# New order tables for the five engines of a gated linear attention and relu-squared kernel

## The chip, the cores and the metric

The kernel runs on one core of a Trainium2 chip. The metric is the device time of one execution in microseconds, here the median of several runs. The five engines have one instruction list each and meet only at semaphores: TensorE (PE in the profile; its weight loads are the row PEld), VectorE (DVE), ScalarE (ACT), GpSimd (POOL) and SyncE (SP), which here only issues DMAs.

## The reference

Two layers are computed one behind the other. The first is a gated linear attention, a recurrence over the tokens; the second is a dense layer pair with a squared relu between:

```python
for t in range(S):                       # B, H, S, D = 4, 8, 768, 48
    state = alpha[:, :, t, :, None] * state + np.einsum('bhd,bhe->bhde', k[:, :, t], v[:, :, t])
    y[:, :, t] = np.einsum('bhd,bhde->bhe', q[:, :, t], state)
x = y.transpose(0, 2, 1, 3).reshape(3072, 384)
h = x @ w_in                             # 384 x 2048
r = np.maximum(h, 0.0)
out = (r * r) @ w_out                    # 2048 x 384
```

Inputs and output are float32; q, k, v and alpha have the shape 4 x 8 x 768 x 48.

## The kernel before

The tokens are cut into units of 256: four batches by three pieces, twelve units, the first pieces of all batches first. A unit g passes through these steps. In the tables the names carry the unit, and often a half or a block behind it, so that sq4_3 is the squaring of unit 4 that ends with block 3.

- **Loads.** lda, ldk, ldq, ldv fetch alpha, k, q and v (384 KB each, L460) into one of four RAW buffers. SyncE issues all of them but those of unit 2, which GpSimd issues, as it does the weights: win0, win1, wout0, wout1 (L433). ldv1 waits for q of unit 0, win for alpha of unit 1, unit 2's loads for v of unit 1, and unit 3's for wout0.
- **Front.** Unit 0 works by halves of the heads: ln0_0 and ln1_0 take logarithms (L476), m10_0 and m11_0 sum them on TensorE (L482 to L488), ei, ea and ec are exponentials, ekm and eqm scale k and q (L512), tr and et transpose them through PSUM (L524, L531, L533). Unit 1 works by token: ln1 (L538), m11 (L542 to L548), ei1, ea1, ec1, ekm1 (L643), eqm (L638), tr0_1 and tr1_1 (L666) with the evictions et0_1 and et1_1 (L674 on VectorE, L676 on ScalarE). From unit 2 on: pr multiplies alphas by pairs (L567 on VectorE, L569 on GpSimd), ln is its logarithm (L570), m1i and m1s sum on TensorE (L576), bk and aq (L594, L596, L605) and lm, lb, es make the other decays, ekm and eqm follow, and from unit 3 on two DMA transposes issued by SyncE, tr0 and tr1 (L654), put them in place. vc is v as bfloat16 (L633 on GpSimd, L634 on ScalarE).
- **Attention.** p0_g are the score matmuls (L874) with the state products (L727). mk0 and mk1 mask them (L891); sa, sc and sd carry the state from one unit of a batch to the next (L825 or L827, L837, L847). y is the output (L754, L762), xe and xf evict it (L908, L910), xt transposes it, on TensorE for units 0 to 3 (L926, with xv as its eviction, L938 or L940), by DMA from unit 4 on (L932).
- **Dense layers.** s1_g_u is one of eight blocks of the first layer (six matmuls, L989) into a hidden PSUM bank. re is the relu (L997 on ScalarE, L999 on VectorE), sq squares two blocks at once, or one for the last two (L1007 on VectorE, L1010 on GpSimd, L1011 on ScalarE). s2_g_j_s is a quarter of the second layer for one half of the unit's tokens (four matmuls, L1035), oe evicts it (L1042, L1044) and out stores it (L1051). The last unit ends with L950, L955, L957 and L958.

A hidden bank is used again two blocks later, or three where psO helps in units 0 and 1, so a block's matmuls wait for the relu of an earlier one.

The order is written out by hand in TABLES: one list of names for each engine. `arrange` (L86) gives every operation to the engine in whose list it stands; many have forms for several engines. `place` (L122) works out which waits are left, and `emit` (L173) writes each list as it stands. So an operation that isn't ready holds all that stands behind it in its list. A name like +512 is a filler: a matmul of a zero tile with 512 columns into psO (L1083), which stands among the first operations of TensorE's list.

Of the kernel before, what the change touches and what calls it, by code (L numbers as in the profile page):

```python
# [204 lines left out]

TABLES = {
    "act": """
        table ln0_0 ln1_0 ei0_0 xcaus ea0_0 ei1_0 ea1_0 ec1_0 et00_0 ec0_0 vc0 ln1 et01_0 et11_0 ei1 ea1 xe0 xv0
# [4 lines left out]
        re4_3 vc6 xe5 lm7 ln7 re4_7 oe3_1 re4_4 ei7 ea7 ec7 re4_6 sq4_6 es7 oe4_0 re5_0 re5_1 lm8 ln8 xe6 re5_2
        re5_3 ei8 ea8 re5_4 re5_5 es8 re5_6 re5_7 sq5_7 re6_0 re6_1 re6_2 vc8 oe5_0 xe7 lm9 ln9 re6_5 re6_6
        oe5_1 re6_7 ei9 ea9 es9 oe6_0 vc9 re7_0 lm10 re7_1 ln10 xe8 re7_3 ei10 ea10 re7_4 re7_5 es10 re7_6 re7_7
        re8_0 oe7_0 re8_1 re8_2 lm11 ln11 xe9 re8_3 re8_4 ei11 ea11 re8_5 re8_6 sq8_5 es11 sq8_7 re9_0 oe8_0
        vc11 re9_1 oe8_1 xe10 re9_3 re9_4 re9_5 re9_6 re9_7 re10_0 oe9_0 re10_1 re10_2 xe11 oe9_1 re10_3 re10_4
# [8 lines left out]
        oe1_1 sd3 sq2_7 sq2_6 xf3 lb5 ekm5 eqm1_5 eqm0_5 sa4 mk1_4 mk0_4 re3_2 pr6 sc4 sq3_1 xf4 sq3_3 re3_5
        sq3_6 lb6 ekm6 sa5 mk0_5 sc5 mk1_5 eqm0_6 eqm1_6 oe3_0 xf5 sq4_1 re4_5 pr7 sq4_3 sq4_7 sq4_5 bk7 lb7
        eqm0_7 sa6 eqm1_7 ekm7 sc6 sd6 mk0_6 mk1_6 pr8 oe4_1 xf6 sq5_3 bk8 lb8 ekm8 sq5_5 sq5_6 sa7 mk0_7 sc7
        mk1_7 eqm0_8 eqm1_8 sq6_1 re6_3 sd7 sq6_3 pr9 xf7 re6_4 sq6_5 sq6_6 sq6_7 bk9 lb9 ekm9 eqm0_9 eqm1_9
        mk0_8 sa8 mk1_8 oe6_1 pr10 sq7_1 xf8 re7_2 sq7_3 bk10 lb10 sq7_5 ekm10 sq7_6 sq7_7 sa9 mk0_9 eqm0_10  # L230
        eqm1_10 mk1_9 pr11 oe7_1 xf9 sq8_3 bk11 lb11 ekm11 sq8_6 re8_7 sa10 mk0_10 eqm0_11 eqm1_11 mk1_10 re9_2
        sq9_1 xf10 sq9_3 sq9_5 sq9_6 sa11 sq9_7 mk0_11 mk1_11 sq10_1 xf11 sq10_3 sq10_5 sq10_6 sq10_7 sq11_1
        sq11_3 sq11_5 sq11_6 sq11_7 oe11_11
    """,
    "pe": """
        +512 +512 +512 +512 +512 +512 +512 +512 m10_0 m11_0 +512 +512 +256 +256 tr00_0 +512 +256 tr10_0 +512
        +256 +256 tr01_0 p0_0 tr11_0 kv0 +512 +512 +512 +256 +256 p1_0 m11 +512 +256 y0 +512 +512 +256 tr0_1 xt0
# [4 lines left out]
        s2_1_1_3 y3 m1i5 s2_2_0_0 s2_2_0_1 xt3 s2_2_0_2 s2_2_0_3 s1_3_0 p0_4 s2_2_1_0 s2_2_1_1 s2_2_1_2 s2_2_1_3
        s1_3_2 s1_3_1 y4 s1_3_4 s1_3_3 m1i6 s1_3_6 s1_3_5 s2_3_0_0 s2_3_0_1 s1_3_7 p0_5 s2_3_0_2 s1_4_0 s1_4_1
        s2_3_0_3 s1_4_2 s1_4_3 y5 s2_3_1_0 s1_4_5 s2_3_1_1 s2_3_1_2 s1_4_7 s2_3_1_3 s1_4_4 m1i7 s2_4_0_0 s1_4_6
        s2_4_0_1 s2_4_0_2 p0_6 s2_4_0_3 s1_5_1 s1_5_0 s2_4_1_0 s2_4_1_1 s1_5_2 s2_4_1_2 s2_4_1_3 y6 s1_5_3 m1i8
        s2_5_0_0 s1_5_4 s1_5_5 s2_5_0_1 s1_5_6 s1_5_7 p0_7 s2_5_0_2 s1_6_0 s1_6_1 s2_5_0_3 s1_6_2 s1_6_3 y7
# [868 lines left out]
```

## Time and profile before

| | |
|---|---|
| median of 3 runs | 174.84 us |
| lowest, highest | 172.93, 175.71 us |
| span of the profiled execution | 171.8 us |
| time of the profiled execution | not given beside its span |
| TensorE, VectorE, ScalarE, GpSimd busy | 165.6, 118.2, 108.9, 24.2 us |
| bytes read, written | 25.17, 4.72 MB |
| granted TensorE clock, mean | 1.000 |

The page's DMA row shows the sixteen DMA engines busy at nine tenths or more almost without a break up to some 130 us, and little after that:

```
DMA  5999999999999999998999998999999582050012
```

Times in the views are microseconds from the start of the span; each row gives start, duration, engine, line and operation, tiles, shapes, and in a bracket how long the engine was idle before and what ended that.

### The profile page before, as it was taken

Reading aid. Unit: us, or ns where it says so; the run is one execution under the profiler, and the core shown is the slowest. Engines: PE = TensorE matmul, PEld = TensorE weight load, DVE = VectorE, ACT = ScalarE, POOL = GpSimd, SP = SyncE. Lnnn points to the kernel's source line nnn. Section 1 sums busy time; section 2 is a strip of 40 time slices with the busy share of each in tenths; the row PEclk is TensorE's granted clock in tenths of the full one; section 3 lists DMA queues with packets and bytes.
Section 4 is the critical chain, followed back from the end, with each engine's and each line's share of the span. In section 5 each row is a group of like instructions: output and inputs, shape, how many; then the busy total and the mean of one; then the engine's idle time right before and its main releaser. Section 6 shows DMA issues by size and latency. Waiting matters only on the chain.

```text
span 171.8 us, 5397 instructions
## 1 busy us (share of the span) xinstructions
PE 165.6 (96%) x2377; PEld 128.9 (75%) x2377; DVE 118.2 (69%) x207; ACT 108.9 (63%) x210; POOL 24.2 (14%) x33
## 2 busy tenths in 40 slices
PE   7999999999999999999999999999999999999994
...
DMA  5999999999999999998999998999999582050012
GB/s 143 323 298 186 260 316 219 245 245 288 182 234 209 269 173 211 305 217 146 288 168 211 267 192 153 337 178 243 255 211 205 81 103 85 0 141 0 22 69 92
DMA packets 74743, 33.37 MB, mean 194 GB/s; under 512 B 71648, under 2 KB 71904, under 8 KB 74720
## 3 DMA queue, kind: packets, MB, share of 16 engines
...
q0 software_dynamic: 1536, 4.72, 12.4%
...
HBM read 25.17 MB, written 4.72 MB: 174 GB/s over the span
## 4 chain that ended last, share of the span: by engine, by line
PE 58%; DMA 20%; SPq 7%; DVE 6%; ACT 4%; POOL 2%; issue 2%; DVEq 0%
PE psWH L989 25%; PE psO L1035 24%; DMA raw<-in_alpha_dram 7%; DMA wout<-in_moe_w_out_dram 6%; DMA raw<-in_q_dram 4%; SPq L460 3%; DMA raw<-in_k_dram 3%; SPq L654 3%; PE psX L950 2%; POOL raw L460 2%; DVE pm L891 1%; PE psZ L762 1%; PE psX L874 1%; DVE qks L638 1%; DVE qks L643 1%
## 5 line engine op out<-in xcount | busy, mean ns | idle before, releaser
L989 PE MATMUL psWH<-xt,win 128*128 128x256 bf16 x552 | 70.9, 274 | 0.4 <-ACT rr L997 0.3
L989 PEld LDWEIGHTS psWH<-xt,win 128*128 128x128 bf16 x552 | 63.2, 144 | 5.2 <-ACT rr L997 1.1
L1035 PE MATMUL psO<-wout,gt 128*128 128x384 bf16 x352 | 66.7, 326 | 0.0
L997 ACT ACTIVATE rr<-psWH 128x512 bf16<-128x512 f32 x79 | 46.8, 597 | 24.4 <-PE psWH L989 22.9
L1035 PEld LDWEIGHTS psO<-wout,gt 128*128 128x128 bf16 x352 | 32.7, 98 | 16.7 <-DMA wout<-in_moe_w_out_dram 0.2
L1007 DVE TENSOR_TENSOR gt<-rr 128x1024 bf16<-128x1024 bf16 (+1 forms) x46 | 26.6, 584 | 22.0 <-ACT rr L997 21.9
L891 DVE TENSOR_TENSOR pm<-psZ,caus 128x1024 bf16<-128x1024 f32 x12 | 14.6, 1218 | 4.7 <-PE psWH L727 4.1
L1042 ACT ACTIVATE osb<-psO 128x384 f32<-128x384 f32 x17 | 8.3, 491 | 11.7 <-PE psO L1035 11.3
L891 DVE TENSOR_TENSOR pm<-psX,caus 128x1024 bf16<-128x1024 f32 x12 | 14.6, 1218 | 1.0 <-PE psX L874 0.5
L1010 POOL TENSOR_TENSOR gt<-rr 128x1024 bf16<-128x1024 bf16 x3 | 5.7, 1894 | 58.7 <-ACT rr L997 58.7
L643 DVE TENSOR_TENSOR qks<-raw,ek 128x768 bf16<-128x768 f32 x11 | 10.5, 952 | 3.0 <-DMA raw<-in_k_dram 2.5
L638 DVE TENSOR_TENSOR qks<-raw,eq 128x384 bf16<-128x384 f32 x22 | 11.4, 553 | 1.7 <-ACT eq L613 1.0
L1083 PE MATMUL psO<-zero 128*128 128x512 bf16 (+1 forms) x33 | 9.1, 407 | 1.3 <-DVE zero L382 1.3
L999 DVE TENSOR_SCALAR rr<-psWH 128x512 bf16<-128x512 f32 x13 | 8.9, 687 | 1.6 <-PE psWH L989 1.4
L1011 ACT ACTIVATE gt<-rr 128x512 bf16<-128x512 bf16 (+1 forms) x11 | 9.1, 823 | 0.7 <-DVE rr L999 0.4
L910 DVE CAST xbf<-psZ 128x384 bf16<-128x384 f32 x10 | 5.5, 554 | 3.2 <-PE psZ L754 3.2
L634 ACT ACTIVATE vbf<-raw 128x768 bf16<-128x768 f32 x7 | 5.9, 843 | 2.2 <-DMA raw<-in_v_dram 2.1
L567 DVE TENSOR_TENSOR prd<-raw 128x384 f32<-128x384 f32 x9 | 5.7, 636 | 2.1 <-DMA raw<-in_alpha_dram 2.0
L609 ACT ACTIVATE la<-raw 128x384 f32<-128x384 f32 x8 | 4.2, 524 | 4.5 <-DMA raw<-in_alpha_dram 4.5
L570 ACT ACTIVATE lab<-prd 128x384 bf16<-128x384 f32 x10 | 5.2, 521 | 2.4 <-DVE prd L567 2.3
L847 POOL TENSOR_TENSOR sbd<-tmp,acm 128x192 bf16<-128x192 f32 x5 | 2.9, 583 | 25.8 <-DVE tmp L837 22.7
L908 ACT ACTIVATE xbf<-psX 128x384 bf16<-128x384 f32 x11 | 5.3, 482 | 1.9 <-PE psZ L754 1.9
...
## 6 DMA issues: line engine op xcount, KB each, us to landing
...
```

The costliest lines, as they stand in the source:

```text
L460: load_op[g, nm] = add(ring, lambda e, dst=dst, src=src: e.dma_start(dst, src), cost, (L_PRIO[g] + j if ring == "sp" else W_PRIO[2] + 10 * ...
L638: add("dve", lambda e, j=j, dst=dst: e.tensor_tensor(dst, RAW[r][:, 2, :, j, :].rearrange("p (n x) d -> p n x d", x=2), EQ[la][:, j].rearr ...
L643: add("dve", lambda e, a=a, E=E: e.tensor_tensor(QKS[qs][:, a, :, :, 0:D], RAW[r][:, 1 + a].rearrange("p h j d -> p j h d"), E[la][:].rear ...
L891: add("dve", lambda e, hf=hf, psT=psT: e.tensor_tensor(PM[pm][:, hf].rearrange("p r n j t -> p (r n) (j t)"), psT[:, :, :].rearrange("p r ...
L989: ins = pe.matmul(psN[:, i * T:(i + 1) * T], WIN[:, kk, hidden(fj)], mov, start=(kk == 0), stop=(kk == KT - 1))
L997: add("act", lambda e, psN=psN, rr=rr: e.activation(rr, psN, AF.Relu), act_ns(512), pu + 600, reads=[keyN], writes=[("rr", rb, half)], nam ...
L999: alts={"dve": (lambda e, psN=psN, rr=rr: e.tensor_scalar(rr, psN, 0.0, None, ALU.max), dve_ns(512))})
L1007: add("dve", lambda e, dst=dst, sq=sq: e.tensor_tensor(dst, sq, sq, ALU.mult), 148 + k * 267, pu + 1200, reads=[("rr", rb, h) for h in ran ...
L1011: "act": (lambda e, dst=dst, sq=sq: e.activation(dst, sq, AF.Square), act_ns(k * 512))})
L1035: ins = pe.matmul(psS, GT[gt][:, fj, j, :], WOUT[:, fj, :], start=(fj == 0), stop=(fj == FT - 1))
L1042: add("act", lambda e, j=j, psS=psS: e.activation(OSB[ob][:, j], psS, AF.Copy), act_ns(DM), ps_ + 700, reads=[keyS], writes=[("osb", ob, j ...
L1083: pr.arrange(TABLES, lambda n: lambda pe: pe.matmul(psO[:, 0:n], ZERO[:, 0:128], ZERO[:, 0:n], skip_group_check=True), zero)
```

## The change

Only the five lists change. All operations stay, with the same 33 fillers (23 of 512 columns, 10 of 256). 45 operations go from ScalarE to VectorE and 36 from VectorE to ScalarE; 25 go from VectorE to GpSimd and 7 from ScalarE to GpSimd; 6 go from GpSimd to VectorE and 2 from GpSimd to ScalarE. Every DMA stays on its queue, SyncE's or GpSimd's, but its place in it can change. The diff, cut to the lines spoken of below:

```diff
     "act": """
-        table ln0_0 ln1_0 ei0_0 xcaus ea0_0 ei1_0 ea1_0 ec1_0 et00_0 ec0_0 vc0 ln1 et01_0 et11_0 ei1 ea1 xe0 xv0
-        ec1 vc1 sa1 re0_0 re0_1 sq0_1 re0_3 xe1 re0_4 re0_5 ln2 re0_6 sq0_6 ei2 ea2 ec2 vc2 re1_2 es2 re1_3
+        table ln0_0 ei0_0 ln1_0 ea0_0 ei1_0 ea1_0 et00_0 et10_0 ec0_0 xcaus ec1_0 ln1 et01_0 et11_0 ei1 ea1 ec1
+        xe0 et0_1 vc1 et1_1 re0_0 re0_3 re0_2 xf1 re0_4 ln2 sq0_1 ei2 re0_6 ea2 sq0_6 re1_0 ec2 re1_3 es2 re1_4
...
     "dve": """
-        eqm0_0 ekm1_0 eqm1_0 et10_0 mk0_0 sa0 mk1_0 ekm1 eqm0_1 eqm1_1 sc0 et0_1 et1_1 mk1_1 mk0_1 sc1 re0_2 xf1
-        sq0_3 pr2 xv1 sq0_5 re0_7 re1_0 re1_1 ekm2 sq0_7 aq2 eqm0_2 eqm1_2 re1_5 et1_2 sq1_1 sq1_5 re1_7 mk1_2
-        pr3 sq1_7 sc2 mk0_2 bk3 eqm1_3 ekm3 aq3 pr4 eqm0_3 xv2 bk4 lb4 ekm4 eqm1_4 eqm0_4 sq2_1 mk1_3 mk0_3 sc3
...
+        ekm1_0 eqm1_0 mk0_0 sa0 zlb1 mk1_0 ekm1 eqm1_1 eqm0_1 sc0 xv0 sa1 mk0_1 mk1_1 re0_1 xe1 pr2 zlb0 sc1 xv1
+        re0_5 re0_7 bk2 eqm1_2 ekm2 re1_1 re1_2 aq2 sd1 sq1_1 eqm0_2 et1_2 re1_7 sa2 sq1_5 mk1_2 sc2 mk0_2 xe2
+        oe0_1 sd2 aq3 eqm1_3 eqm0_3 ekm3 bk4 lb4 ekm4 eqm0_4 eqm1_4 oe1_1 mk0_3 sc3 mk1_3 sd3 sq2_6 xf3 lb5 xv3
...
     "pe": """
-        +512 +512 +512 +512 +512 +512 +512 +512 m10_0 m11_0 +512 +512 +256 +256 tr00_0 +512 +256 tr10_0 +512
-        +256 +256 tr01_0 p0_0 tr11_0 kv0 +512 +512 +512 +256 +256 p1_0 m11 +512 +256 y0 +512 +512 +256 tr0_1 xt0
-        tr1_1 +512 +512 +512 +512 +512 +256 p0_1 s1_0_0 s1_0_1 s1_0_3 s1_0_2 y1 s1_0_4 s1_0_5 xt1 s1_0_6 s1_0_7
-        m1i2 s1_1_0 s1_1_1 s1_1_2 m1s2 s1_1_3 s1_1_4 tr0_2 s1_1_6 s1_1_5 tr1_2 s2_0_0_0 s1_1_7 p0_2 s2_0_0_1
...
+        +256 +512 +512 +256 +512 +256 +512 +256 +512 +512 +512 +512 +512 +512 m10_0 +256 +512 +512 +512 m11_0
+        +512 tr00_0 tr10_0 +512 +256 tr01_0 +512 p0_0 tr11_0 +256 +256 kv0 +512 p1_0 m11 +512 +512 +256 +512 y0
+        +256 +512 tr0_1 +512 xt0 tr1_1 +512 p0_1 s1_0_0 s1_0_3 s1_0_1 s1_0_2 y1 s1_0_4 xt1 s1_0_6 s1_0_5 m1i2
+        s1_0_7 s1_1_0 s1_1_1 s1_1_2 s1_1_3 m1s2 tr0_2 s1_1_4 s1_1_6 s1_1_5 s2_0_0_0 tr1_2 s1_1_7 s2_0_0_1 p0_2
...
     "pool": """
-        slinc slstr sident scaus scaus1 win0 win1 lda2 sd0 ldq2 ldv2 ldk2 wout0 sd1 wout1 bk2 sd2 sq2_3 vc4 pr5
-        bk5 sd4 vc5 bk6 sd5 sq5_1 vc7 sq8_1 vc10
+        scaus1 slinc slstr sident scaus vc0 win0 win1 lda2 ldk2 ldq2 ldv2 wout0 sq0_3 wout1 sq0_5 sd0 vc2 sq1_3
+        sq0_7 sq1_6 pr3 pr4 bk3 pr5 sq2_1 vc4 sq2_3 sq2_7 bk5 pr6 sd4 vc5 sq4_3 vc6 sq4_5 pr8 vc7 sq6_1 sq6_3
+        sd7 pr10 vc9 pr11 sd6 sq8_3 bk11 vc11 sq9_3 sq10_1 sq10_3 sq10_7 sq11_1
     """,
     "sp": """
-        lda0 ldk0 ldq0 ldv0 lda1 ldk1 ldv1 ldq1 lda3 ldk3 ldq3 lda4 ldv3 ldk4 ldq4 ldv4 tr0_3 tr1_3 lda5 tr0_4
-        out0_1 tr1_4 ldk5 ldq5 ldv5 lda6 ldk6 tr1_5 tr0_5 out2_1 xt4 ldq6 out1_1 ldv6 lda7 ldq7 ldk7 tr0_6 tr1_6
-        xt5 ldv7 out3_1 lda8 ldk8 tr0_7 tr1_7 out4_1 xt6 ldq8 ldv8 lda9 ldq9 ldk9 tr0_8 tr1_8 xt7 ldv9 lda10
...
+        lda0 ldk0 ldq0 ldv0 lda1 ldq1 ldv1 ldk1 lda3 lda5 lda4 ldk3 ldq3 ldq4 ldv4 ldv3 ldk4 tr1_3 tr0_3 out0_1
+        tr1_4 tr0_4 ldk5 ldq5 lda6 ldk6 ldv5 out1_1 tr1_5 tr0_5 xt4 out2_1 ldq6 lda7 ldv6 ldk7 ldq7 tr0_6 tr1_6
+        xt5 ldv7 lda8 ldk8 out3_1 tr0_7 tr1_7 xt6 out4_1 lda9 ldq8 ldv8 ldk9 ldq9 tr1_8 tr0_8 xt7 lda10 ldv9
...
```

More of the change, by code (lines that the diff above doesn't have):

```diff
@@ L213 @@
[L213 to L217, printed above, removed]
@@ new lines @@
+        oe2_1 xf4 xe4 ei6 re3_4 lm6 ea6 ec6 sq3_3 re3_6 sq3_5 sq3_6 re3_7 es6 re4_0 sq3_7 re4_2 re4_3 xe5 ln7
+        re4_5 ei7 ea7 ec7 lm7 oe3_1 sq4_7 sq4_6 oe4_0 es7 re5_0 re5_2 re5_1 lm8 ln8 xe6 sq5_1 re5_4 ei8 ea8
+        re5_5 re5_7 sq5_6 sq5_7 oe5_0 re6_0 re6_1 es8 lm9 ln9 re6_3 ei9 vc8 xf7 ea9 re6_4 re6_5 oe5_1 re6_6
+        re6_7 oe6_0 es9 ln10 ei10 re7_2 ea10 xf8 oe6_1 lm10 re7_4 xe8 sq7_5 re7_6 sq7_7 sq7_6 oe7_0 re8_1 re8_0
+        es10 re8_2 ln11 xf9 re8_4 vc10 re8_5 re8_6 lm11 re8_7 ei11 sq8_7 ea11 re9_0 oe8_0 es11 re9_1 re9_3 sq9_1
@@ L220 @@
+        re9_2 re9_4 xf10 re9_6 sq9_6 re10_1 re10_3 re10_2 xe11 sq10_5 re10_7 re10_6 re11_1 re11_3 re11_4 sq11_3
+        sq11_5 sq11_6 sq11_7
     """,
     "dve": """
-        zero zlinc zlstr zident zcaus zcaus1 zla0 zla1 zones zown zown0 zown1 zqk0 zqk1 zqk2 zlb0 zlb1 ekm0_0
-        eqm0_0 ekm1_0 eqm1_0 et10_0 mk0_0 sa0 mk1_0 ekm1 eqm0_1 eqm1_1 sc0 et0_1 et1_1 mk1_1 mk0_1 sc1 re0_2 xf1
-        sq0_3 pr2 xv1 sq0_5 re0_7 re1_0 re1_1 ekm2 sq0_7 aq2 eqm0_2 eqm1_2 re1_5 et1_2 sq1_1 sq1_5 re1_7 mk1_2
@@ L225 @@
-        pr3 sq1_7 sc2 mk0_2 bk3 eqm1_3 ekm3 aq3 pr4 eqm0_3 xv2 bk4 lb4 ekm4 eqm1_4 eqm0_4 sq2_1 mk1_3 mk0_3 sc3
[L226 to L233, printed above, removed]
+        zero zlinc zlstr zident zcaus zcaus1 zla0 zla1 zones zown zown0 zown1 zqk0 zqk1 zqk2 ekm0_0 eqm0_0
+        ekm1_0 eqm1_0 mk0_0 sa0 zlb1 mk1_0 ekm1 eqm1_1 eqm0_1 sc0 xv0 sa1 mk0_1 mk1_1 re0_1 xe1 pr2 zlb0 sc1 xv1
@@ L242 @@
[L242 to L246, printed above, removed]
@@ new lines @@
+        +256 +512 tr0_1 +512 xt0 tr1_1 +512 p0_1 s1_0_0 s1_0_3 s1_0_1 s1_0_2 y1 s1_0_4 xt1 s1_0_6 s1_0_5 m1i2
+        s1_0_7 s1_1_0 s1_1_1 s1_1_2 s1_1_3 m1s2 tr0_2 s1_1_4 s1_1_6 s1_1_5 s2_0_0_0 tr1_2 s1_1_7 s2_0_0_1 p0_2
+        s2_0_1_0 s2_0_1_1 s2_0_0_2 s2_0_1_2 s2_0_0_3 m1i3 s2_0_1_3 y2 s2_1_0_0 m1s3 xt2 s2_1_0_1 s2_1_0_2 m1i4
+        s1_2_0 s1_2_1 s2_1_0_3 s1_2_2 s1_2_3 s2_1_1_0 s2_1_1_1 s1_2_4 s1_2_5 s2_1_1_2 s2_1_1_3 p0_3 s2_2_0_0
+        s1_2_7 s1_2_6 m1i5 s2_2_0_1 y3 s2_2_0_2 xt3 s2_2_0_3 p0_4 s2_2_1_0 s1_3_0 s1_3_1 s2_2_1_1 s2_2_1_2
@@ new lines @@
+        s2_6_0_3 p0_8 s2_6_1_0 s1_7_1 s1_7_0 s2_6_1_1 s1_7_3 s2_6_1_2 s1_7_2 m1i10 y8 s2_6_1_3 s1_7_4 s1_7_5
+        s2_7_0_0 s1_7_6 s1_7_7 s2_7_0_1 p0_9 s2_7_0_2 s2_7_0_3 s1_8_1 s1_8_0 s2_7_1_0 s1_8_3 s2_7_1_1 s2_7_1_2
+        s1_8_2 s2_7_1_3 y9 m1i11 s1_8_4 s1_8_5 s2_8_0_0 s1_8_6 s2_8_0_1 s1_8_7 p0_10 s2_8_0_2 s1_9_0 s2_8_0_3
+        s1_9_1 s1_9_2 s2_8_1_0 s1_9_3 s2_8_1_1 s2_8_1_2 s2_8_1_3 s1_9_4 y10 s2_9_0_0 s1_9_5 s1_9_6 s2_9_0_1
+        s1_9_7 p0_11 s2_9_0_2 s1_10_0 s1_10_1 s2_9_0_3 s1_10_2 s1_10_3 y11 s2_9_1_0 s2_9_1_1 s1_10_4 s1_10_5
@@ L267 @@
+        ldk10 tr1_9 tr0_9 out5_1 out6_1 xt8 ldq10 lda11 ldk11 ldv10 tr0_10 tr1_10 xt9 ldv11 ldq11 tr1_11 tr0_11
+        xt10 out7_1 out8_1 xt11 out10_1 out9_1 out11_0 out11_10 out11_11
     """,
```

35 lines of the change are left out of this document (17 added, 18 removed).

## The prediction

> **What bounds the kernel now.** I read the page's head first, with the busy shares and the chain of waits by engine, then the busy time by stage (stretch, its length, then TensorE's busy time), then the rests ahead of single TensorE instructions.
>
> ```profile
> span 171.8 us, 5397 instructions
> ...
> PE 165.6 (96%) x2377; PEld 128.9 (75%) x2377; DVE 118.2 (69%) x207; ACT 108.9 (63%) x210; POOL 24.2 (14%) x33
> ...
> PE 58%; DMA 20%; SPq 7%; DVE 6%; ACT 4%; POOL 2%; issue 2%; DVEq 0%
> ```
> ```profile
> 140.00:150.00 10.00, 10.00 (x161) 7.97 (x160) 5.70 (x9) 4.80 (x9) 0.00 (x0) 1.00 0.22 61
> ```
>
> The 96% count the fillers of the start as work. The useful dense stretch begins with the scores of unit 1 (p0_1, at 17.32, below). From there TensorE hardly rests; the stage from 140 to 150 is full. Every rest after 17.32 that the timeline marks on TensorE is here, picked from several stretches, with the idle time in the bracket:
>
> ```profile
> 21.94 1.51 PE L989 MATMUL psWH<-xt,win 128*128 128x256 bf16 x12 [0.32 <-ACT rr L997]
> 41.49 0.34 PE L576 MATMUL psWH<-lab,linc 128*128 128x384 bf16 x1 [0.17 <-ACT lab L570]
> 61.52 0.37 PE L762 MATMUL psZ<-vbf,pm 64*128 64x48 bf16 x16 [0.38 <-DVE pm L891]
> 80.83 0.38 PE L874 MATMUL psX<-kqt 64*64 64x128 bf16 x13 [0.40 <-ACT eq L613]
> 88.80 0.34 PE L576 MATMUL psWH<-lab,linc 128*128 128x384 bf16 x1 [0.24 <-ACT lab L570]
> ```
>
> They add up to 0.32 + 0.17 + 0.38 + 0.40 + 0.24 = 1.51 us. Over a quarter of the chain of waits is DMA and SyncE's queue, but with rests this small TensorE's own work bounds the kernel from 17.32 on. The change keeps every matmul, so an order can win these 1.5 us and what it takes off the start; it can lose any amount by letting TensorE wait.
>
> **Part 1, the start.** Both versions issue 33 fillers, but ahead of unit 0's first decay sum m10_0 there were eight of 512 columns and now there are ten of 512 and four of 256, in width 12 for 8. The rows are picked from the timelines of TensorE, ScalarE and VectorE:
>
> ```profile
> 1.26 3.59 PE L1083 MATMUL psO<-zero 128*128 128x512 bf16 x8 [1.26 <-DVE zero L382]
> 4.94 0.26 PE L482 MATMUL psX<-laf,linc 128*128 128x192 bf16 x1
> 9.31 0.84 ACT L538 ACTIVATE laf<-raw 128x768 bf16<-128x768 f32 x1 [0.34 <-DMA raw<-in_alpha_dram]
> 10.00 1.04 PE L1083 MATMUL psO<-zero 128*128 128x512 bf16 x5
> 14.43 0.62 PE L666 MATMUL psZ<-ident,qks 128*128 128x128 bf16 x8
> 17.32 0.42 PE L874 MATMUL psX<-kqt 64*64 64x128 bf16 x16
> 16.19 0.84 ACT L634 ACTIVATE vbf<-raw 128x768 bf16<-128x768 f32 x1
> 29.38 1.02 ACT L676 ACTIVATE kqt<-psZ 128x1024 bf16<-128x1024 bf16 x1
> 31.26 0.68 DVE L674 COPY kqt<-psZ 128x1024 bf16<-128x1024 bf16 x1
> ```
>
> The eight took 3.59 / 8 = 0.45 us each and ended at 4.85, 0.09 before m10_0, so nothing covers four more. Later fillers take 1.04 / 5 = 0.21 us. The added four cost 4 x 0.21 = 0.83, less the 0.09, so 0.7 us, if the fast pace holds from 4.85; at 0.45 they cost 1.7. I take 0.7, and keep 1.7 for the range. The Trainium skill (TensorE: Matmul & The Clock Gate, Part 1) says that the slow pace lasts for a time of some 3.4 us of activity and not for a number of matmuls, give or take 0.5 us by the phase of a free-running window; by it the added fillers run mostly fast, which is the 0.7, or in a late phase up to 1.7; the trace agrees so far as eight took 3.59 us and all later ones ran fast.
>
> ScalarE passes the 0.7 on: ei0_0 now stands ahead of ln1_0, and et10_0 came over, so ln1 (L538, 9.31) is reached some 0.7 us later, and with it et11_0, p1_0, m11 and the front of unit 1. Then the two evictions et0_1 and et1_1 move from VectorE (0.68 each) to ScalarE (1.02 each), with the cast vc1 (0.84) between them. The rows for the two forms are those of unit 2's evictions. The first can start at the end of tr0_1, 14.43 + 0.62 + 0.7 = 15.75; 1.02 + 0.84 + 1.02 with two overlaps of 0.1 ends at 18.43, and p0_1 starts near 18.48 in place of 17.32: **+1.15 us**. The second half of win hides some of it:
>
> ```profile
> 9.58 1.71 POOL L433 DMA_DIRECT2D win<-in_moe_w_in_dram  x2 [6.64 <-DMA raw<-in_alpha_dram]
> DMA to landing us min/median/max: 8.5/9.9/11.3
> ```
>
> Issued near 10.5, the second piece lands 11.3 later, at 21.8; the idle 0.32 us ahead of 21.94 is this transfer (the bracket names a relu that had long ended), and a late TensorE no longer waits for it. Net **+0.85 us**.
>
> **Part 2, work moved to GpSimd.** Thirty-two operations come to GpSimd, eight leave; fourteen squarings of 1,024 columns stand there where there were three. TensorE waits for them only through GT, with slack. The price is what they do to VectorE:
>
> ```profile
> 122.56 1.89 POOL L1010 TENSOR_TENSOR gt<-rr 128x1024 bf16<-128x1024 bf16 x1 [34.92 <-ACT rr L997]
> 124.40 1.15 POOL L633 CAST vbf<-raw 128x768 bf16<-128x768 f32 x1
> 123.58 1.30 DVE L567 TENSOR_TENSOR prd<-raw 128x384 f32<-128x384 f32 x1 [0.41 <-DMA raw<-in_alpha_dram]
> 23.20 0.56 DVE L567 TENSOR_TENSOR prd<-raw 128x384 f32<-128x384 f32 x1 [0.39 <-DMA raw<-in_alpha_dram]
> 84.98 1.90 POOL L1010 TENSOR_TENSOR gt<-rr 128x1024 bf16<-128x1024 bf16 x1 [14.42 <-ACT rr L997]
> 85.19 1.22 DVE L891 TENSOR_TENSOR pm<-psZ,caus 128x1024 bf16<-128x1024 f32 x1
> ```
>
> The product pr11 started 0.88 us before GpSimd's squaring ended at 124.45, and took 1.30 in place of 0.56: it stood still until then. The mask at 85.19, whose first input is PSUM, ran beside a squaring at its usual 1.22. And vc10, up at 124.40, took 1.15 behind pr11, whose last 0.47 us it met. So a VectorE operation with both inputs in SBUF doesn't run beside one of GpSimd, and a squaring there can hold one of VectorE for up to 1.9 us. Three places where that decides, with the rows that show how much lies between VectorE's result and TensorE's use of it today (ln2 and m1i2; ekm2 and tr0_2; eqm0_2 with eqm1_2, and tr1_2):
>
> ```profile
> 23.98 0.52 ACT L570 ACTIVATE lab<-prd 128x384 bf16<-128x384 f32 x1
> 24.94 0.33 PE L576 MATMUL psWH<-lab,linc 128*128 128x384 bf16 x1
> 27.36 0.95 DVE L643 TENSOR_TENSOR qks<-raw,ek 128x768 bf16<-128x768 f32 x1
> 28.68 0.61 PE L666 MATMUL psZ<-ident,qks 128*128 128x128 bf16 x8
> 29.15 1.03 DVE L638 TENSOR_TENSOR qks<-raw,eq 128x384 bf16<-128x384 f32 x2
> 30.45 0.61 PE L666 MATMUL psZ<-ident,qks 128*128 128x128 bf16 x8
> ```
>
> (a) sq0_3 on GpSimd starts when re0_2 ends; y1, xe1 and then pr2 follow, so that pr2 comes up about 0.7 us later (an estimate from these steps' lengths) and waits the other 1.2. The log ln2 (23.98) and m1i2 (24.94) stand behind; between the end of the log and m1i2 lie 24.94 - 24.50 = 0.44 today, and VectorE's xv1 and re0_5 are late too, so about 0.6 of the 1.2 reach TensorE. (b) sq0_5 starts at the end of re0_5; bk2, now on VectorE ahead of ekm2, waits about 1.0, and ekm2 feeds tr0_2 with 28.68 - 28.31 = 0.37 between them today: 0.6 is not covered, with re1_1 and re1_2 queued behind, whose hidden banks s1_1_4 and s1_1_5 need: 0.3 more. (c) sq1_3, sq0_7 and sq1_6 (1.89, and two of half the columns, 0.95 each as an estimate from it) meet aq2, sd1, sq1_1 and eqm0_2, and eqm0_2 feeds tr1_2, with 0.27 between them today. If VectorE's queued operations go first, (c) costs nothing and the sum is 1.5; if GpSimd's go in between each time, (b) grows by 0.9 and (c) costs about 2.9, together 5.3. Pr11 got going at 124.45 though vc10 was up at 124.40, so the row is nearer to VectorE first: I take **2.3**, and keep 0 (if all is covered) and 5.3 for the range.
>
> **Part 3, the loads.** On SyncE lda5 moves ahead of lda4, ldk3 and ldq3, one more 384 KB transfer before them:
>
> ```profile
> 35.00 2.24 SPq L460 DMA_DIRECT2D raw<-in_v_dram  x1
> 39.62 1.28 SPq L460 DMA_DIRECT2D raw<-in_v_dram  x1
> 41.38 4.00 SPq L654 DMA_TRANSPOSE kqt<-qks  x2
> 80.67 0.58 SPq L1051 DMA_DIRECT2D out_dram<-osb  x1
> 50.61 1.00 POOL L569 TENSOR_TENSOR prd<-raw 128x384 f32<-128x384 f32 x1 [1.87 <-DMA raw<-in_alpha_dram]
> ```
>
> A load takes 1.3 to 2.2 us of the queue, so ekm3, eqm0_3, eqm1_3 and the transposes of 41.38 come that much later. Behind these transposes wait out0_1 and the transposes of unit 4, which p0_3 and p0_4 need. But p0_3 stands two groups later in TensorE's list (some 1.5 us, as the pair at 21.94), and TensorE is late by 0.85 + 2.3 there anyway: zero; without that cover up to 0.7. Likewise k5. lda8 passes out3_1 (80.67, 0.58), while pr8 behind it goes to GpSimd (1.00 for 0.56, +0.44): the two nearly cancel. A late TensorE absorbs rests that hang on transfers, at most 0.17 + 0.38 + 0.40 + 0.24 = 1.19; since the transposes wait for VectorE too, I count half: **-0.6**.
>
> **The rest at nothing.** Forty-five operations go from ScalarE to VectorE and 36 back, mostly relus and evictions. The relu of a hidden bank is wanted only by the second next group, and both engines are idle for 31% and 37% of the span, which hides them; where one stands behind a held operation, that is (b). The last groups of TensorE, the store and its landing stay as they are.
>
> **Sum.** 0.85 + 2.3 - 0.6 = 2.55, so a span of 174.35. The three runs of before were 172.93 to 175.71, median 174.84, that is 1.1 to 3.9 and in the median 3.04 above the profiled span; the time of the profiled execution itself isn't given. 174.35 + 3.04 = **177.4**.
>
> **The rivals.** *GpSimd in turn* (0.28): every queued GpSimd operation gets in between VectorE's. 0.85 + 5.3 - 0.6 = 5.55, so **180.4**. For it speaks that the trace nowhere shows two queues of such operations side by side; against it, pr11's row. The Trainium skill (SBUF — State Buffer, Who interferes with whom) says that whoever issues first has the shared pair for the whole instruction; that rule would lead to taking turns; the trace agrees on the standstill (0.88 us at 123.58) and is silent on two queues. *Covered* (0.20): the held operations have more slack than I count, so 0.85 - 0.6 = 0.25 and **175.1**; for it speaks VectorE's idle 31%. *Faster* (0.10): lda8 and ldk8 ahead of the store, and alpha of unit 5 early, end the rests of 41, 61, 80 and 88 us in full while the start is not late: 171.8 - 1.5 = 170.3, so **173.3**. It decides at ln1: if that starts within 0.3 us of its 9.31, this holds; my own walk has it 0.7 late. My forecast, VectorE mostly first, has 0.42.
>
> **Chances and range.** A 2% change is 3.5 us, about what this measurement can tell. Faster by that would take 171.3, more than all rests give: 0.03. Slower by that is *in turn* and the upper end of the forecast: 0.32. Within: 0.65. The low end is *covered* with all 1.19 absorbed, 174.5, less 0.7 for the spread of the runs, 173.8; the high end is *in turn* with part of the slow fillers, 181.2.
>
> **What would show it.** m10_0 near 5.6, p0_1 near 18.5, and s1_0_4 without a rest; pr2 and bk2 at 1.3 us or more beside GpSimd squarings; rests of TensorE ahead of m1i2, tr0_2 and tr1_2 (a matmul list that stands still where the three places say). I am wrong if pr2 takes 0.56, or if p0_1 is on time.

## The result and the profile after

The changed kernel takes **185.75 us** (median of four runs, 185.12 to 186.51), the kernel before 173.88 (172.93 to 175.71). The ratio is 1.074, with a 95% interval of 1.066 to 1.082: slower by 7.4%, above the range that ended at 181.2. The ratio leaves out one run of before that fell into a slower state, 175.71 us, so its base is 172.93 us. Below, a point is one per cent of that, 1.7 us. The profiled execution took 185.12 us with a span of 183.4. So 1.7 us lie outside the span; the prediction had counted 3.04 for it, because the three runs of before had a median a good 1 us above what this gives. That was a small error upwards.

The head of the page after, with the chain of waits by engine in the last line:

```profile
span 183.4 us, 5399 instructions
PE 167.6 (91%) x2374; PEld 129.6 (71%) x2377; DVE 128.6 (70%) x197; ACT 102.7 (56%) x196; POOL 62.4 (34%) x57
...
PE 61%; DVE 16%; ACT 9%; DMA 7%; issue 3%; SPq 2%; DVEq 0%
```

GpSimd's busy time went from 24.2 to 62.4 us. VectorE's rose by 10.4 although it lost more operations than it gained (207 instructions before, 197 now), and its share of the chain went from 6% to 16%, while DMA fell from 20% to 7%. The same reading by groups: the products of q with its decay, which no list moved to another engine, cost half as much again. The rows give busy time and mean ns; before first, then after:

```profile
L638 DVE TENSOR_TENSOR qks<-raw,eq 128x384 bf16<-128x384 f32 x22 | 11.4, 553 | 1.7 <-ACT eq L613 1.0 <-DMA raw<-in_q_dram 0.6
```
```profile
L637 DVE TENSOR_TENSOR qks<-raw,eq 128x384 bf16<-128x384 f32 x22 | 17.6, 823 | 1.7 <-DMA raw<-in_q_dram 1.7
```

(The tables after are one line shorter, so line numbers there are lower by one.) Rows picked from several stretches of TensorE's timeline after: the start of unit 0's sum (m10_0), p0_1, and then the rests of over 0.6 us with that of m1i2:

```profile
5.63 0.25 PE L481 MATMUL psX<-laf,linc 128*128 128x192 bf16 x1
18.69 0.42 PE L873 MATMUL psX<-kqt 64*64 64x128 bf16 x16 [1.64 <-ACT kqt L675]
26.06 0.34 PE L575 MATMUL psWH<-lab,linc 128*128 128x384 bf16 x1 [0.42 <-ACT lab L569]
31.45 0.62 PE L665 MATMUL psZ<-ident,qks 128*128 128x128 bf16 x8 [1.15 <-DVE qks L642]
37.84 0.62 PE L665 MATMUL psZ<-ident,qks 128*128 128x128 bf16 x8 [2.95 <-DVE qks L637]
58.64 0.82 PE L1034 MATMUL psO<-wout,gt 128*128 128x384 bf16 x4 [0.75 <-DVE osb L1043]
63.74 0.51 PE L925 MATMUL psX<-ident,xbf 128*128 128x128 bf16 x6 [0.67 <-DVE xbf L909]
117.42 0.42 PE L873 MATMUL psX<-kqt 64*64 64x128 bf16 x16 [1.52 <-DMA kqt<-qks]
141.83 0.38 PE L873 MATMUL psX<-kqt 64*64 64x128 bf16 x13 [0.89 <-ACT rr L996]
```

The seven rests are m1i2, tr0_2, tr1_2, s2_2_0_0, xt3, p0_8 and p0_10. They add up to 0.42 + 1.15 + 2.95 + 0.75 + 0.67 + 1.52 + 0.89 = 8.35 us; all five rests of before were 1.51. With three small ones that are not shown (0.30, 0.23 and 0.17) TensorE rests 9.05 us behind p0_1. So rests account for 9.05 - 1.51 = 7.5 of the 11.6 us by which the span grew, and the later start of p0_1 (18.69 for 17.32) for 1.4. The first three are the places (a), (b) and (c). Rows picked from the timelines of VectorE, and then of GpSimd, at these places:

```profile
23.67 1.71 DVE L566 TENSOR_TENSOR prd<-raw 128x384 f32<-128x384 f32 x1
27.84 1.27 DVE L595 TENSOR_TENSOR ek<-ek,raw 128x384 f32<-128x384 f32 x1
29.03 0.86 DVE L637 TENSOR_TENSOR qks<-raw,eq 128x384 bf16<-128x384 f32 x1
29.82 1.57 DVE L642 TENSOR_TENSOR qks<-raw,ek 128x768 bf16<-128x768 f32 x1
32.98 2.05 DVE L846 TENSOR_TENSOR sbd<-tmp,acm 128x192 bf16<-128x192 f32 x1
34.95 1.52 DVE L1006 TENSOR_TENSOR gt<-rr 128x1024 bf16<-128x1024 bf16 x1
36.40 1.39 DVE L637 TENSOR_TENSOR qks<-raw,eq 128x384 bf16<-128x384 f32 x1
```
```profile
23.07 1.90 POOL L1009 TENSOR_TENSOR gt<-rr 128x1024 bf16<-128x1024 bf16 x1 [7.04 <-ACT rr L996]
26.81 1.89 POOL L1009 TENSOR_TENSOR gt<-rr 128x1024 bf16<-128x1024 bf16 x1 [1.28 <-DVE rr L998]
28.67 0.81 POOL L846 TENSOR_TENSOR sbd<-tmp,acm 128x192 bf16<-128x192 f32 x1
29.43 1.15 POOL L632 CAST vbf<-raw 128x768 bf16<-128x768 f32 x1
32.67 4.70 POOL L1009 TENSOR_TENSOR gt<-rr 128x1024 bf16<-128x1024 bf16 x3 [2.09 <-DVE rr L998]
```

Place (c) shows the taking of turns best: three squarings back to back on GpSimd (32.67 to 37.37), and beside them three operations on VectorE, each of which had to let one squaring pass. The carry sd1 took 2.05 us, sq1_1 1.52 and eqm0_2 1.39, and tr1_2 begins 0.05 us after the last. At (b) bk2 waits for the squaring, eqm1_2 for GpSimd's sd0, ekm2 for its cast vc2: three holds in a row.

### The profile page after: what moved, and what is told of

It reads as the page before. It is cut to its first block, busy times and chain, and to the rows that moved or that the text cites. A ratio compares the mean times of both kernels' runs of the same rounds, so it can differ in the third digit from the quotient of the medians.

```text
span 183.4 us, 5399 instructions
## 1 busy us (share of the span) xinstructions
PE 167.6 (91%) x2374; PEld 129.6 (71%) x2377; DVE 128.6 (70%) x197; ACT 102.7 (56%) x196; POOL 62.4 (34%) x57
## 3 DMA queue, kind: packets, MB, share of 16 engines
q0 software_dynamic: 1536, 4.72, 11.6%
## 4 chain that ended last, share of the span: by engine, by line
PE 61%; DVE 16%; ACT 9%; DMA 7%; issue 3%; SPq 2%; DVEq 0%
PE psO L1034 22%; PE psWH L988 22%; DMA kqt<-qks 5%; DVE qks L637 4%; PE psO L1082 3%; DVE pm L890 3%; ACT rr L996 3%; DMA raw<-in_k_dram 3%; PE psX L873 2%; DVE prd L566 2%; DVE qks L642 2%; PE psWH L1034 2%; SPq L653 2%; PE psX L949 1%; PE psZ L761 1%
## 5 line engine op out<-in xcount | busy, mean ns | idle before, releaser
L996 ACT ACTIVATE rr<-psWH 128x512 bf16<-128x512 f32 x61 | 35.8, 598 | 31.1 <-PE psWH L988 30.7
L1009 POOL TENSOR_TENSOR gt<-rr 128x1024 bf16<-128x1024 bf16 (+1 forms) x18 | 32.2, 1795 | 54.3 <-ACT rr L996 47.0
L998 DVE TENSOR_SCALAR rr<-psWH 128x512 bf16<-128x512 f32 x31 | 21.0, 685 | 11.1 <-PE psWH L988 10.9
L1010 ACT ACTIVATE gt<-rr 128x512 bf16<-128x512 bf16 (+1 forms) x25 | 20.0, 815 | 10.7 <-DVE rr L998 10.4
L568 POOL TENSOR_TENSOR prd<-raw 128x384 f32<-128x384 f32 x7 | 8.1, 1160 | 31.5 <-DMA raw<-in_alpha_dram 31.5
L637 DVE TENSOR_TENSOR qks<-raw,eq 128x384 bf16<-128x384 f32 x22 | 17.6, 823 | 1.7 <-DMA raw<-in_q_dram 1.7
L1006 DVE TENSOR_TENSOR gt<-rr 128x1024 bf16<-128x1024 bf16 (+1 forms) x17 | 12.7, 762 | 5.1 <-ACT rr L996 5.1
L873 PE MATMUL psX<-kqt 64*64 64x128 bf16 x192 | 5.2, 229 | 4.7 <-DMA kqt<-qks 1.8
L1043 DVE COPY osb<-psO 128x384 f32<-128x384 f32 x10 | 5.5, 554 | 5.0 <-PE psO L1034 2.9
L632 POOL CAST vbf<-raw 128x768 bf16<-128x768 f32 x7 | 7.6, 1081 | 2.3 <-DMA raw<-in_v_dram 2.3
```

The source lines that it names most:

```text
L637: add("dve", lambda e, j=j, dst=dst: e.tensor_tensor(dst, RAW[r][:, 2, :, j, :].rearrange("p (n x) d -> p n x d", x=2), EQ[la][:, j].rearr ...
L873: ins = pe.matmul(psT[64 * c:64 * c + 64, rr_, o:o + 128], keys, mov)
L996: add("act", lambda e, psN=psN, rr=rr: e.activation(rr, psN, AF.Relu), act_ns(512), pu + 600, reads=[keyN], writes=[("rr", rb, half)], nam ...
L998: alts={"dve": (lambda e, psN=psN, rr=rr: e.tensor_scalar(rr, psN, 0.0, None, ALU.max), dve_ns(512))})
L1006: add("dve", lambda e, dst=dst, sq=sq: e.tensor_tensor(dst, sq, sq, ALU.mult), 148 + k * 267, pu + 1200, reads=[("rr", rb, h) for h in ran ...
L1009: alts={"pool": (lambda e, dst=dst, sq=sq: e.tensor_tensor(dst, sq, sq, ALU.mult), 200 + k * 840), "act": (lambda e, dst=dst, sq=sq: e.act ...
```

## The experiments

Lists are shown as the edit of names; order and all else stay. Comparisons by ratio are against the kernel before on the same chip.

**e1: the five early squarings off GpSimd.** On the kernel after:

```diff
 pool: ... wout0 -sq0_3 wout1 -sq0_5 sd0 vc2 -sq1_3 -sq0_7 -sq1_6 pr3 ...
 act:  ... ec2 +sq0_3 re1_3 es2 +sq0_5 re1_4 re1_5 re1_6 et0_2 +sq0_7 +sq1_3 +sq1_6 sq1_7 ...
```

> The changed kernel with five squarings of units 0 and 1 (sq0_3, sq0_5, sq0_7, sq1_3, sq1_6) taken off GpSimd and given to ScalarE; nothing else differs. Theory HOLD (a GpSimd operation that reads SBUF and a VectorE operation with two SBUF inputs exclude each other, and take turns): TensorE's rests ahead of m1i2 (0.58), tr0_2 (1.31) and tr1_2 (3.12) shrink to under 0.4 each, with them the slow-clock stretch behind 39 us (1.5 us), and ScalarE's extra work costs up to 1 us: 179 to 181 us, first place for bk2 near 0.55 us. Rival ORDER (the new places of loads, relus and evictions cost the time, the holds are hidden anyway): 184 to 186.5 us, with the rest ahead of p0_3 and later stages taking over what goes here.

Measured: 180.77 us, ratio 1.048 (1.042 to 1.055). Five operations that TensorE hardly waits for are worth 2.6 points. VectorE's timeline has sd1 at 0.35 us where it took 2.05, and in TensorE's tr1_2 follows the matmul ahead of it without a rest (no bracket):

```profile
31.49 0.35 DVE L846 TENSOR_TENSOR sbd<-tmp,acm 128x192 bf16<-128x192 f32 x1
```
```profile
33.33 0.44 PE L665 MATMUL psZ<-ident,qks 128*128 128x128 bf16 x5
```

**e3: idle squarings in the kernel before.** Nobody reads what they write:

```diff
+    add("dve", fill(DUMI[:], 1.0), 300, -1e6, writes=[("dumi",)], name="zdum")
+    for i in range(5):
+        add("pool", lambda e: e.tensor_tensor(DUMO[:, 0:1024], DUMI[:], DUMI[:], ALU.mult), ..., name=f"dum{i}")
 pool: ... sd1 wout1 +dum0 +dum1 bk2 +dum2 +dum3 +dum4 sd2 ...
```

> The kernel before with nothing moved, and five squarings of a constant tile (128x1024, 1.9 us each) added to GpSimd's list where GpSimd is idle, two behind wout1 and three behind bk2; nobody waits for them (one fill of the constant tile is added to VectorE's list before unit 0). HOLD: VectorE's sq0_3, pr2, sq0_5, ekm2, aq2 and eqm of unit 2 are held, pr2 takes over 1.5 us in place of 0.56, TensorE rests ahead of m1i2 and tr0_2 or tr1_2, and the kernel takes 178 to 182 us. ORDER: GpSimd's idle work costs nothing, 173 to 175 us.

**e4: the same with five fills.**

```diff
+        add("pool", lambda e: e.memset(DUMO[:], 0.0), ..., name=f"dum{i}")
```

> The same with fills (128x2048 bfloat16, no input) in place of the five idle squarings. If a GpSimd operation holds VectorE only by reading SBUF: 173 to 175 us and every pr2 and eqm at its usual length. If any GpSimd operation that uses SBUF holds VectorE: up to as slow as the one before, scaled by the length of a fill. ORDER: 173 to 175 us.

Measured: **181.18 us** with the squarings, ratio 1.048 (1.041 to 1.054); **172.32 us** with the fills, ratio 0.999 (0.995 to 1.003). Rows picked from the timelines of VectorE and GpSimd, with squarings and then with fills:

```profile
29.86 2.46 DVE L648 TENSOR_TENSOR qks<-raw,ek 128x768 bf16<-128x768 f32 x1
32.24 2.11 DVE L1012 TENSOR_TENSOR gt<-rr 128x512 bf16<-128x512 bf16 x1
34.27 2.24 DVE L610 TENSOR_TENSOR eq<-eq,raw 128x384 f32<-128x384 f32 x1
29.61 6.50 POOL L442 TENSOR_TENSOR dumo<-dumi 128x1024 bf16<-128x1024 bf16 x3
```
```profile
26.94 0.95 DVE L648 TENSOR_TENSOR qks<-raw,ek 128x768 bf16<-128x768 f32 x1
26.79 5.52 POOL L442 MEMSET dumo<- 128x2048 bf16 x3
```

Three squarings and three operations of VectorE lie side by side again, one for one: 2.46, 2.11 and 2.24 us where 0.95, 0.42 and 0.55 are usual. The fills keep GpSimd busy for nearly as long (5.52 for three) and hold nobody. So the price is neither GpSimd's time nor a wait on a semaphore but the reading of SBUF. The Trainium skill (SBUF — State Buffer, Who interferes with whom) says just this: a VectorE instruction with two SBUF inputs contends with a GpSimd instruction that reads SBUF, not with one that only writes. Here 181.18 against 172.32 us bears it out.

**e13: only place (c) taken away.** In the kernel after sq0_7, sq1_3 and sq1_6 go to ScalarE behind et0_2; sq0_3 and sq0_5 stay.

> The kernel after with the three squarings of place (c), sq0_7, sq1_3 and sq1_6, on ScalarE behind et0_2; sq0_3 and sq0_5 stay on GpSimd. IN TURN theory: the rest of 3.12 us ahead of tr1_2 goes, those of 0.58 at m1i2 and about 1.31 at tr0_2 stay, and the run is 3 to 3.5 us shorter than the kernel after: 182.3 to 182.8 us, and e1's further 1.5 us belong to the places (a) and (b). Rival: the early places share one slack, so that taking one away only lengthens the next: under 1.5 us won, above 184.3 us.

Measured: 182.73 us, ratio 1.058 (1.052 to 1.064), so 1.6 points for (c) and the other 1.0 of e1 for (a) and (b). TensorE's rests show the same split; the one ahead of tr1_2 (35.41) is gone, that of tr0_2 is as it was:

```profile
32.13 0.62 PE L665 MATMUL psZ<-ident,qks 128*128 128x128 bf16 x8 [1.15 <-DVE qks L642]
...
35.41 0.61 PE L665 MATMUL psZ<-ident,qks 128*128 128x128 bf16 x8
```

**e2: all squarings and eight products off GpSimd.** e1, and thirteen more squarings to ScalarE; pr3, pr4, pr6, pr8, pr10, pr11, bk3 and bk11 to VectorE.

> As the one before, and the other thirteen squarings off GpSimd too (to ScalarE, at the places in time where GpSimd had them), and six pair products and two bk back to VectorE; GpSimd keeps its casts, decays of the state, pr5 and bk5. HOLD: the rests ahead of s2_2_0_0 (0.82), xt3 (0.84), m1i7 (0.39), p0_8 (1.59) and p0_10 (0.96) go as well: 175.5 to 178 us, the late start (1.4 us) being what is left. ORDER: 182 us or more.

Measured: 181.42 us, ratio 1.051 (1.046 to 1.056), no better than e1, and in neither theory's range. Four of the five rests that HOLD named are gone in its trace, and p0_10's is 0.72. But my list brought in waits of its own. The first is in VectorE's timeline: pr3 needs alpha of unit 3 and stands ahead of the eviction et1_2, and pr4 behind that waits for its own alpha (1.24). TensorE then rests 1.51 us ahead of s2_0_1_0, for a relu behind pr4, and 1.37 ahead of p0_3, for the cast vc3, which stands behind two of the added squarings on ScalarE:

```profile
34.85 0.56 DVE L567 TENSOR_TENSOR prd<-raw 128x384 f32<-128x384 f32 x1 [1.47 <-DMA raw<-in_alpha_dram]
```
```profile
38.46 1.47 PE L1035 MATMUL psWH<-wout,gt 128*128 128x384 bf16 x8 [1.51 <-DVE rr L999]
...
54.94 0.42 PE L874 MATMUL psX<-kqt 64*64 64x128 bf16 x16 [1.37 <-ACT vbf L634]
```

So the run neither prices the later holds nor speaks against them; an operation can't just be handed to another engine: its place in that list has a price too.

**e6: the later holders.** e1, and sq2_3, sq2_7, sq4_3, sq6_1 and sq6_3 to ScalarE, pr11 to VectorE, lm9 behind ln9.

> e1 and in addition sq2_3, sq2_7, sq4_3, sq6_1 and sq6_3 on ScalarE, pr11 on VectorE, lm9 behind ln9. HOLD theory: the rests at s2_2_0_0 (0.80), xt3 (0.84), m1i7 (0.46), m1i9 (1.03), p0_8 (1.19) and p0_10 (0.89) go, 5.2 us in all, and the run takes 175.5 us. Rival (next in line): behind each hold another wait ends nearly as late, so that less than half of the 5.2 us is won: above 178.2 us.

Measured: 177.61 us, ratio 1.029 (1.019 to 1.038): 2.0 points less than e1, or 3.4 us where 5.2 were expected. (The swap of lm9 and ln9 is no hold, and it was not tried alone.) What the holders had done in the kernel after, VectorE then GpSimd:

```profile
54.77 3.35 DVE L637 TENSOR_TENSOR qks<-raw,eq 128x384 bf16<-128x384 f32 x2
...
108.97 2.75 DVE L637 TENSOR_TENSOR qks<-raw,eq 128x384 bf16<-128x384 f32 x2
```
```profile
55.50 2.20 POOL L1009 TENSOR_TENSOR gt<-rr 128x1024 bf16<-128x1024 bf16 x1
...
106.50 4.02 POOL L1009 TENSOR_TENSOR gt<-rr 128x1024 bf16<-128x1024 bf16 x2 [9.59 <-ACT rr L996]
```

Two products that take 1.03 us as a pair took 3.35 and 2.75. The second pair feeds DMA transposes, and p0_8 then rests 1.52 us for a transfer; in e6 it does not rest. Part of the gain was lost again at a relu that stands behind sq6_3 on ScalarE, by my own edit:

```profile
106.22 1.53 PE L988 MATMUL psWH<-xt,win 128*128 128x256 bf16 x12 [0.67 <-ACT rr L996]
```

**e5, e14, e11: the start.** e5 is e1 with the instructions up to p0_1 as in the kernel before; e14 is the kernel after with that start; e11 is the kernel before with the start of the kernel after.

```diff
 act (e5, e14): table ln0_0 ln1_0 ei0_0 xcaus ea0_0 ei1_0 ea1_0 ec1_0 et00_0 ec0_0 ln1 et01_0 et11_0 ei1 ea1 ec1 xe0 vc1 ...
 dve (e5, e14): ... eqm1_0 +et10_0 mk0_0 ... sc0 +et0_1 +et1_1 xv0 ...
```

> The five squarings are on ScalarE as in e1, and the instructions up to p0_1 stand on TensorE, ScalarE and VectorE as in the kernel before. START theory: the start costs what its first layer norms and its fillers cost, p0_1 begins at about 17.4 us instead of 19.30 in e1, nothing behind it changes, and the run is 1.9 us shorter than e1: 178.9 us. Rival (absorbed): the time won at the start is lost again in front of the loads, p0_1 begins earlier but the rests grow by as much, and the run stays at 180.8 us.

> The kernel after, all its GpSimd work included, with the start of the kernel before up to p0_1. SUM theory: p0_1 at 17.4 instead of 18.69, and the run 0.85 to 1.4 us shorter, 184.4 to 184.9 us. ABSORBED theory, from e5: the chains of the places (a) to (c) stand behind loads that land at 24 to 27 us whenever the start ends; the run stays within 0.5 us of the kernel after.

> The kernel before with the start of the kernel after: TensorE's list up to p0_1 with its fillers, ScalarE's list through et1_1, vc0 on GpSimd. The prediction's Part 1: p0_1 about 1.15 us later and the run 0.85 us longer (0.3 of it won back at a load). ABSORBED theory, from e5: p0_1 comes 1.2 to 2 us later, but the loads and chains of the first two iterations end where they ended, less than half of it is left behind 50 us, and the run is 0 to 0.6 us longer than before.

Measured: e5 180.84 us, ratio 1.048 (1.039 to 1.057), the same as e1, although p0_1 begins at 17.50 in place of e1's 19.30: later p0_8 and p0_10 rest 1.62 and 2.00 us where they rest 1.12 and 0.82 in e1. e14 184.99 us, 1.072 (1.065 to 1.080), 0.2 points under the kernel after, which is nothing by these intervals; e11 175.91 us, 1.017 (1.011 to 1.024). In e14 TensorE:

```profile
17.52 0.42 PE L873 MATMUL psX<-kqt 64*64 64x128 bf16 x16 [0.59 <-DVE xt L937]
...
36.76 0.62 PE L665 MATMUL psZ<-ident,qks 128*128 128x128 bf16 x8 [2.95 <-DVE qks L637]
```

Here p0_1 is 1.17 us earlier than in the kernel after and tr1_2 still 1.08, so the loads of 24 to 27 us did not absorb the start there, which I had expected. The executions of e14 range from 183.16 to 185.72. The profiled one is the shortest and the only one with a mean granted clock of 1.000; the three others have 0.991. The intervals leave anything from nothing to the predicted size open. In e11 the start alone costs the kernel before 3 us, far over the prediction's 0.85, but the edit isn't a clean copy: xv0, which the change gives to VectorE, stays on ScalarE behind the two evictions, and p0_1 waits for it. The profiled execution took 176.43 us, and behind this rest its clock was halved for 3.4 us:

```profile
20.38 0.42 PE L874 MATMUL psX<-kqt 64*64 64x128 bf16 x16 [2.25 <-ACT xt L940]
```

So the start's share is 0, 0.2 and 0.7 points by e5, e14 and e7 (below), each good to about one point; e11 has a wait that the kernel after does not have, and so does not price it.

**e8: the rest ahead of tr1_2 filled.** Behind the longest rest the granted clock was halved for one stretch of the profiled execution. Thirteen fillers of 512 columns (`pe: ... s2_0_0_0 +warm tr1_2 ...`) go into the kernel after.

> The kernel after with 13 fillers of 512 columns on TensorE ahead of tr1_2, where it rests 3.1 us. REST theory: the half clock of 3.4 us that follows comes from that rest; with the rest filled the granted clock stays full, the products p0_2, s2_0_1_0 and s2_0_1_1 do not trail, and the run is 1.5 us shorter than the kernel after: 184.2 us. Rival: the half clock comes from something else (the load of the start, the first wide products); the run stays at 185.7 us or is longer by what the fillers push.

Measured: 186.29 us, ratio 1.080 (1.070 to 1.089). Busy time by stage, after and then e8 (stretch, its length, TensorE's busy time, its weight loads, VectorE, ScalarE, GpSimd, granted clock, DMA share, GB/s):

```profile
35.61:39.02 3.41, 1.18 (x15) 1.17 (x16) 2.69 (x3) 0.66 (x1) 3.41 (x4) 1.00 1.01 272
39.02:42.43 3.41, 3.41 (x72) 2.07 (x71) 1.42 (x4) 1.04 (x2) 0.59 (x1) 0.50 1.14 314
```
```profile
39.00:42.40 3.40, 3.40 (x82) 2.26 (x81) 2.59 (x5) 1.04 (x2) 0.73 (x1) 1.00 1.17 318
```

With TensorE busy through the rest the clock stayed at 1.00, as the REST theory has it; all four executions of e8 have a mean clock of 1.000. The 1.5 us did not come off the time. Nor does the half clock show in the time of the kernel after: its executions with it (mean clock 0.991) took 185.12 and 185.85 us, those without 185.65 and 186.51. In e8's profile as much is lost again at a transposed tile that a DMA brings, a rest that the kernel after did not have there:

```profile
131.94 1.31 PE L994 MATMUL psWH<-xt,win 128*128 128x256 bf16 x10 [1.87 <-DMA xt<-xbf]
```

**e7 and e15: what is left.** e7 joins e5 and e6. e15 takes two waits out of e7 that its own edits had made: sq0_7 goes to ScalarE behind sq0_5, and sq6_3 to VectorE behind eqm1_8.

> e5 and e6 together. If the start and the holds are separate terms that add up, 180.8 - 1.9 - 5.2 = 173.7 us, within 1 us of the kernel before on the same chip. Rival: there is a third part in the change (load order, order of TensorE's list) that costs 2 us or more by itself: above 175.5 us.

> e7 with its own two new waits taken away: sq0_7 on ScalarE earlier, behind sq0_5, and sq6_3 on VectorE behind eqm1_8. The rests at s2_0_1_0 (0.63) and s1_6_6 (0.84) go: 1.5 us less than e7, about 1.3 per cent over the kernel before instead of 2.2. Rival: they are replaced by others, no change from e7.

Measured: e7 176.63 us, ratio 1.022 (1.015 to 1.029); e15 175.69 us, 1.015 (1.009 to 1.022). e15 is 0.7 points under e7 (0.9 expected) and 1.5 over the kernel before. The 0.7 is not clear of nothing by these intervals. I found no single cause of the 1.5: e15's trace marks six rests of TensorE behind p0_1, 0.17 to 0.66 us long and at different kinds of waits, and at (b) eqm1_2 still takes 1.18 us beside the cast vc2.

**e9 and e10: the orders of loads and of TensorE alone.** e9 is the kernel before with SyncE's list of the kernel after (and unit 2's loads in its order). e10 is the kernel before with TensorE's list of the kernel after from p0_1 to s2_4_1_0 and from m1i10 to p0_11.

> The kernel before with the order of loads, transposes and stores of the kernel after (SyncE's whole list, and lda2's three companions on GpSimd); everything else stays. The prediction's Part 3 says nothing: within 0.7 us of before on the same chip. Rival (third part): e7 still lost 2.7 us of TensorE's time to before without its holds and with before's start; if that comes from the order of the loads, this run is 1.5 to 2.7 us slower.

> The kernel before with TensorE's order of the kernel after, from p0_1 through s2_4_1_0 and from m1i10 through p0_11 (between and behind them before's order, since VectorE's and ScalarE's lists of before cannot follow it there). If TensorE's order costs nothing by itself: within 0.7 us of before. Rival (third part): the order asks for products earlier than the unchanged engines deliver them, 1 to 2 us slower.

Measured: e9 174.63 us, ratio 1.016 (1.010 to 1.021); e10 189.97 us, 1.103 (1.098 to 1.108). Neither is the price of that part in the kernel after. In e9 the loads of unit 3 now land behind that of alpha of unit 5; eqm1_3 waits 3.14 us for its q, before's VectorE list has the product pr4 behind it, and m1i4 stands still:

```profile
41.20 0.56 DVE L638 TENSOR_TENSOR qks<-raw,eq 128x384 bf16<-128x384 f32 x1 [3.14 <-DMA raw<-in_q_dram]
...
44.18 0.34 PE L576 MATMUL psWH<-lab,linc 128*128 128x384 bf16 x1 [2.73 <-ACT lab L570]
```

In the kernel after pr4 is on GpSimd and m1i4 has no rest. In e10 the second layer of unit 2 is asked for before VectorE, in before's order, has evicted what lies in its bank:

```profile
58.19 1.40 PE L1035 MATMUL psO<-wout,gt 128*128 128x384 bf16 x4 [3.29 <-DVE osb L1044]
```

One list out of five, or most of it, put among the four others' old orders, costs 1.6 to 10%. The five lists are one order, and a part of it cannot be priced by moving it alone.

**e12: an attempt at a faster kernel.** The kernel before, with ldk5 ahead of out0_1, ldk7 behind tr1_6, lda8 and ldk8 ahead of out3_1.

> The kernel before with four loads moved on SyncE: ldk5 ahead of out0_1, ldk7 behind tr1_6, lda8 and ldk8 ahead of out3_1. TensorE's rests of 0.47 us at p0_6 and 0.47 at m1i8 end with chains that begin at the landing of ldk7 and lda8. If these loads set them, 0.5 to 1 us shorter than before; rival: another chain ends as late, no change within 0.5 us.

Measured: 172.81 us, ratio 1.003 (0.999 to 1.006): no change, though in its profile m1i8 and p0_6 have no rest. None of these kernels beats the kernel before.

## Why the prediction was wrong

The direction was right, and so was the standstill that the prediction saw in Part 2: of the 7.4 points 2.6 come off with the five early squarings and 2.0 more with six later holders, 4.6 together. e15's 0.7 would come on top as gains of the same removals, but they are not clear of nothing. What failed is the order in which two queues go, and with it the size, in three steps.

**The choice between the two bounds of Part 2 failed.** "VectorE mostly first", 2.3 us, was taken from the row of pr11, and the rival *GpSimd in turn*, 5.3 us, was right: the three rests are 0.42 + 1.15 + 2.95 = 4.5 us, and e1 gains 2.6 points, 4.5 us. The walk held at two places of three. (a): pr2 was to lose 1.2 us and took 1.71 for 0.56; 0.6 was to reach TensorE, the rest has 0.42. (b): 0.9, and 0.9 more in turn, made 1.8, and the rest is 1.15; bk2 lost 0.71 and not 1.0. (c): 2.9 was to be lost in turn, and the rest is 2.95. The row of pr11 could not decide: there VectorE's operation had waited already while GpSimd's next came up, so its going first was its turn. A row with one waiting operation was read as an order between two queues. On a matter with bounds of 0 and 5.3 and only one row, the end where the mechanism costs most deserved the larger chance. Yet with *GpSimd in turn* the forecast would have been 180.4, still 5 us short; the next step is most of that.

**The places were sized from three, and the rest at nothing.** Thirty-two operations came to GpSimd; the prediction followed five. The later rests, s2_2_0_0, xt3, p0_8 and p0_10, add up to 0.75 + 0.67 + 1.52 + 0.89 = 3.83 us, and e6 won 2.0 points, 3.4 us. So a term of nothing measured 3.4 to 3.8 us. "Forty-five operations ... at nothing", hidden by idle engines, left out that a held VectorE passes the delay to all behind it.

**The absorption of -0.6 happened, and more than its size was lost beside it.** The four rests that a late TensorE was to absorb are all gone in the kernel after: m1i4, y4, p0_6 and m1i8 have no bracket there, 1.19 us. But the term left out that SyncE's transposes wait for the same held products, so that transfers become late too: p0_8 now rests 1.52 us (counted above) for transposes that stand behind the held pair at 108.97. Another 0.30 us for a transpose, at p0_5, I did not follow.

**The start came out as walked in the profiled execution, in part by luck.** m10_0 is at 5.63 (near 5.6 predicted), p0_1 at 18.69 (18.48), and s1_0_4 has no rest. But of the six kept traces with these lists at the start this one has the earliest p0_1; the others have 18.83, 19.30, 19.38, 19.70 and 19.77. In the six the first fourteen fillers took between 4.54 and 5.30 us, and m10_0 is at 5.63 to 6.35, where it was at 4.94 before. So the 0.7 for the added fillers was the low end, and up to 1.4 came of it. The latest p0_1, in e2:

```profile
19.77 0.42 PE L874 MATMUL psX<-kqt 64*64 64x128 bf16 x16 [1.64 <-ACT kqt L676]
```

The start's end-to-end price of 0.85 us, 0.5 points, lies among the 0, 0.2 and 0.7 points of e5, e14 and e7, and these cannot tell it from nothing.

**Part 3 at nothing** stays open. In the kernel after p0_3 and p0_4 do begin without a rest, as it said, but no run prices the loads there: e9's 1.6 points arise with before's VectorE list and do not carry over. Also open is where the last 1.5 points of e15 come from.
